# A decay attention with two expert layers on one core: decays first, pads later, one more pair in plain float32

## The chip, the cores and the metric

The kernel runs on one NeuronCore of a Trainium2 chip. The metric is the device time of one execution in microseconds (us), the median of several runs. Engines are named as in the profile: PE is TensorE (PEld its weight load), DVE VectorE, ACT ScalarE, POOL GpSimd, SP SyncE, which here only starts DMAs. ACT starts some DMAs too; the queues of both are SPq and ACTq in the rows.

## The reference

Batch 4, 8 heads, 576 tokens, head width 64; the float64 weights are 512 x 1536 (two), 1536 x 512, 512 x 1024 and 1024 x 512.

```python
log_f = np.log(np.clip(f, 0.0001, 1.0)); cum = np.cumsum(log_f, axis=-1)
scores = scale * q @ k.T + cum[:, :, :, None] - cum[:, :, None, :]
scores = np.where(causal, -1e9, scores)
attn = np.exp(scores - max) ; attn = attn / (attn.sum() + 1e-9)
x = (attn @ v)                                  # to 2304 tokens x 512
h = ((x @ w_a) * (x @ w_b)) @ w_out             # first layer, 512 -> 1536 -> 512
h = h @ w_in                                    # second layer, 512 -> 1024
solu = h * softmax(h)
out = (solu - mean) / sqrt(var + 1e-6) * g_ln @ w_out2
```

## The kernel before, in words

**An order from a planner.** The kernel describes its work as some thousand operations (`op`: allowed engines with planned durations, a key, what it reads and writes, what it must follow in `after`). `Sched.run` places them: of all engines it takes the one that can start something first, and on it the ready operation with the smallest key. The keys come from the table `Y`: `Z0`, `T0`, `T1`, `TA`, `TF` and `ZD` set the time of each head, `W0`, `WD0` and `WK` those of the pieces of weights, `TE`, `T2`, `EO`, `EL` those of the second layer. Every engine then executes its instructions in that order; a wait at the head of an engine or of a DMA queue holds all that stands behind it. Two costs matter below: an operation counts as ready `LAT` = 0.06 us after what it depends on, and a DMA with a key below `D2` may go on SP's or ACT's queue, whichever ends first.

**Decays** (L563 to L591). `f`, 32 rows of 576, is loaded into `ft`, clipped on DVE (L571), its logarithm taken on ACT (L574), summed on DVE (scan L576, with a tile of ones, `on`, from the memset L570), negated (`cumr`, L580) and its low part made (`cl`, L583). For the first three heads a row of each goes by DMA into the head's `sets` (`load_cum`), for the others over DRAM. The scores read these rows as extra lines of the contraction.

**Attention.** A head loads q, k and v (`four_load`, `four_v`, `pair_load`, `late_v`), transposes q and k on PE (L909), splits them in a rounded high part and a low part (L929 to L944, copies L918), and computes each row's maximum from a first product (`max_scores`, L973; with the causal mask either added by a product of `ident` and `cmask` on PE, L977, or added on DVE, L1000; the maximum then comes from L997). Heads below `PM` and those of the first batch mask on PE. A second product (`scores`, L1047 and L1055) then subtracts the maximum, and ACT takes the exponential. Three kinds of heads exist: `K0` (the first 256 queries of the first batch's heads), `K1` (their other 320 queries) and `KF` (whole heads of the other batches). For `K0` and `K1` the exponentials are multiplied with v in plain float32 (`weigh_whole`, L1136). For `KF` the exponentials (L1167) are masked on POOL (L1176), rounded on ACT (L1183), their low part is made on DVE or POOL (L1189), v is split too (`v_split`), and `weigh` (L1224) runs three products for each piece.

**Weights and first layer.** `load_cols` loads float64 weights in pieces into two buffers and converts them on ACT, DVE and POOL (L659 to L706). `up_unit` (L1356) multiplies a block of tokens with one piece of `w_a` and `w_b`, and the products go to DRAM. `down` (L1650) is the second product of the layer.

**Second layer.** `pair` takes 256 tokens and computes `x @ w_in` by seven products of halves (L1736, buffers of one bank in turn out of three), added up on DVE into `h1` (first 128 tokens) and `h2` (L1747). `rest` then does for each: maximum (L1780), exponential (L1782), product, mean and variance, subtraction (L1794), transposes on PE (L1828), the split of the transposes on ACT (L1831) and DVE (L1834), and the product with `w_out2` (L1843), scaled on the way out (L1853). `h1`, `h2` and the transposes have one buffer each.

**Constants and products of zeros.** POOL makes `ident` and `cmask` (L535); `k_set` fills the constant lines of `sets`, part 0 (first 256 columns) and parts 1 and 2, the pads (L523 to L532); `k_nat` (L515) and `k_vs` (L542) are more of them. After planning, `fill` puts products of `ident` and the zeros of `cmask` (L1901) into PE's planned gaps before `F1`, once both are there; their result is used by nothing.

Of the kernel before, what the change touches and what calls it, by code (L numbers as in the profile page):

```python
# [23 lines left out]
def t_act(n, psum=False):  # L24
    return (0.155 if psum else 0.187) + n / 1200.0
# [22 lines left out]
def t_mm4(ns):  # L48
    return sum(n / 600.0 + 0.05 for n in ns)
# [22 lines left out]
class Sched:  # L72
# [21 lines left out]
    def op(self, opts, key, fn, r=(), w=(), after=(), lat=0.0, port=False, nbytes=0, lean="BIAS"):  # L94
# [11 lines left out]
        for b, p in r:  # L106
            if p in b.last:
# [25 lines left out]
    def run(self, state):  # L133
# [70 lines left out]
        while left:  # L204
# [91 lines left out]
    "Z0": 13.6157,  # L296
    "T0": 4.7453,
    "T1": 5.9693,
    "TA": 10.8799,
    "TF": 18.2246,  # L300
    "U0": 2.8496,
    "U1": 1.2595,
    "UF": 2.1602,
    "UL": 1.1171,
    "LEAD": (1.2959, 6.0955),
    "SHRINK": 1.9433,
    "W0": 39.7443,
    "WD0": 3.1311,
    "WN": 4,
    "WD1": 0.0,  # L310
    "WD2": 11.5154,
    "EZ": 8.5785,
    "EO": 17.4803,
    "TE": 28.6422,
    "DL": 0,
    "BIAS": 0.3295,
    "UO": (7.4065, 7.7289, 10.1476),
    "UD": 26.2153,
    "UK": 375.6785,
    "L3": 14,  # L320
    "TL": (0.0, 0.0),
    "F1": 287.7428,
    "FG": 0.275,
    "FF": 0.7369,
# [32 lines left out]
    "WIN": 0.0,  # L357
# [4 lines left out]
def kernel(  # L362
# [154 lines left out]
    op(("POOL", 0.5), 20.0, k_nat, w=[(CONST, "natpad")])  # L517
# [48 lines left out]
    ft, on, cum = xr(0)[:BH], pfw[:BH, :S], xr(1)[:BH]  # L566
# [1384 lines left out]
```

## Time and profile before

| | us |
|---|---|
| median of 3 runs | 911.74 (910.98 to 911.75) |
| the profiled execution | 911.28 |
| its span, first to last instruction | 909.50 |
| PE busy | 891.7 |
| DVE busy | 616.2 |
| ACT busy | 462.5 |
| POOL busy | 169.4 |

The profile is that of one execution. A matmul's end is modelled, and successive matmuls overlap, so a busy PE is not PE at its peak; products of zeros count as busy. In the rows an instruction of a `...ld` engine is a weight load. What stands in brackets is the idle time of the engine just before, and what ended it. In the chain of waits a row is what the end of the program hung on at that time.

### The profile page before, as it was taken

Reading aid. Unit: us, or ns where it says so; the run is one execution under the profiler, and the core shown is the slowest. Engines: PE = TensorE matmul, PEld = TensorE weight load, DVE = VectorE, ACT = ScalarE, POOL = GpSimd, SP = SyncE. Lnnn points to the kernel's source line nnn. Section 1 sums busy time; section 2 is a strip of 40 time slices with the busy share of each in tenths; the row PEclk is TensorE's granted clock in tenths of the full one; section 3 lists DMA queues with packets and bytes.
Section 4 is the critical chain, followed back from the end, with each engine's and each line's share of the span. In section 5 each row is a group of like instructions: output and inputs, shape, how many; then the busy total and the mean of one; then the engine's idle time right before and its main releaser. Section 6 shows DMA issues by size and latency. Waiting matters only on the chain.

```text
span 909.5 us, 14259 instructions
## 1 busy us (share of the span) xinstructions
PE 891.7 (98%) x5027; PEld 764.0 (84%) x5031; DVE 616.2 (68%) x1198; ACT 462.5 (51%) x869; POOL 169.4 (19%) x297
## 2 busy tenths in 40 slices
PE   8999999999999999999999999999999999999996
PEld 4778877999888888888888888988888888888884
DVE  7868767776746656655664345889587768757784
ACT  4967755767564556563663234655333434243332
POOL 7766743222321224111100000000000000000000
PEclk9999999999999999999999999999999999999999
DMA  7446562333333233322484233442120111111001
GB/s 169 129 127 175 154 180 73 90 90 84 90 87 77 75 90 82 96 61 66 139 272 139 67 119 111 156 151 81 47 70 24 46 59 47 35 49 41 28 25 35
DMA packets 110044, 85.02 MB, mean 93 GB/s; under 512 B 69874, under 2 KB 91508, under 8 KB 109972
## 3 DMA queue, kind: packets, MB, share of 16 engines
q1 hardware_dynamic: 106116, 82.11, 31.4%
q10 hardware_dynamic: 3856, 1.99, 0.9%
q8 instruction: 40, 0.66, 0.3%
q14 instruction: 32, 0.26, 0.1%
HBM read 57.38 MB, written 19.55 MB: 85 GB/s over the span
## 4 chain that ended last, share of the span: by engine, by line
PE 93%; ACT 3%; DVE 2%; DMA 1%; issue 1%; POOL 0%; ACTq 0%; DVEq 0%; SPq 0%
PE ps L1356 32%; PE ps L1650 16%; PE ps L1843 11%; PE ps L1736 9%; PE ps L1224 7%; PE ps L1055 3%; PE ps L973 3%; PE ps L1047 3%; PE ps L1136 2%; PE ps L909 2%; PE ps L1828 2%; PE ps L1901 1%; DMA fw<-in_moe_w_a_dram 1%; DVE mts L997 1%; ACT sets L929 0%
## 5 line engine op out<-in xcount | busy, mean ns | idle before, releaser
L1356 PE MATMUL ps<-xs,wt 128*128 128x256 f32 (+1 forms) x1728 | 327.0, 341 | 0.0
L1356 PEld LDWEIGHTS ps<-xs,wt 128*128 128x128 f32 x1728 | 268.0, 189 | 34.0 <-POOL wt L706 0.3
L1650 PE MATMUL ps<-wt,sets 128*128 128x512 f32 (+1 forms) x420 | 91.8, 370 | 0.0
L1650 PEld LDWEIGHTS ps<-wt,sets 128*128 128x128 f32 x420 | 72.9, 189 | 12.8
L1843 PE MATMUL ps<-wt 128*128 128x512 f32 x324 | 80.3, 393 | 1.8 <-DVE wt L1834 1.0
L1381 DVE TENSOR_TENSOR fw<-ps,fw 128x256 f32<-128x256 f32 (+1 forms) x72 | 40.1, 556 | 58.8 <-PE ps L1356 33.4
L1736 PE MATMUL ps<-wt,xs 128*128 128x512 f32 x306 | 79.3, 392 | 0.0
L1189 DVE TENSOR_TENSOR pexp<-fw,pexp 128x768 fp32r<-128x768 f32 (+1 forms) x46 | 46.3, 1007 | 42.6 <-ACT pexp L1183 41.9
L1843 PEld LDWEIGHTS ps<-wt 128*128 128x128 f32 x324 | 60.0, 188 | 15.1 <-DVE wt L1834 1.9
L1224 PE MATMUL ps<-pexp,VS 128*128 128x448 f32 (+4 forms) x432 | 72.2, 312 | 0.4 <-DVE pexp L1189 0.4
L1638 ACT CAST wt<-nat 128x512 fp32r<-128x512 f32 (+1 forms) x60 | 34.7, 580 | 70.4 <-PE ps L1650 66.2
L1224 PEld LDWEIGHTS ps<-pexp,VS 128*128 128x128 f32 x432 | 65.8, 190 | 4.5 <-DVE pexp L1189 0.5
L1736 PEld LDWEIGHTS ps<-wt,xs 128*128 128x128 f32 x306 | 56.5, 188 | 11.4 <-DVE wt L1834 0.2
L1379 ACT COPY fw<-ps 128x256 f32<-128x256 f32 (+1 forms) x72 | 34.6, 480 | 60.8 <-PE ps L1356 59.0
L1176 POOL TENSOR_SCALAR_AFFINE_SELECT fw<-fw 128x128 f32<-128x128 f32 (+1 forms) x120 | 34.6, 319 | 146.1 <-ACT fw L1167 146.0
L1000 DVE CUSTOM_DVE_ANT_0 ps<-ps,cmask 128x512 f32<-128x512 f32 (+4 forms) x95 | 51.0, 554 | 13.7 <-PE ps L973 12.0
L1642 DVE TENSOR_TENSOR wt<-nat,wt 128x512 fp32r<-128x512 f32 (+1 forms) x60 | 38.0, 634 | 28.1 <-ACT wt L1638 26.9
L1167 ACT ACTIVATE fw<-ps 128x768 f32<-128x768 f32 (+1 forms) x48 | 39.7, 836 | 27.7 <-PE ps L1055 25.7
L1047 PE MATMUL ps<-sets 128*128 128x320 f32 (+4 forms) x200 | 49.6, 295 | 1.8 <-DVE mts L997 1.1
L1248 ACT ACTIVATE xrw<-ps 64x576 f32<-64x576 f32 (+2 forms) x40 | 22.0, 550 | 54.4 <-PE ps L1224 52.1
L1055 PE MATMUL ps<-sets 67*128 67x288 f32 (+6 forms) x200 | 48.9, 320 | 0.0
L973 PE MATMUL ps<-sets 66*128 66x512 f32 (+5 forms) x192 | 45.2, 329 | 0.6 <-ACT sets L929 0.3
(186 smaller groups left out, 1518.1 us busy)
## 6 DMA issues: line engine op xcount, KB each, us to landing
gs<-fw SPq DMA_DIRECT2D x36, 256.0 KB
nat<-gs SPq DMA_DIRECT2D x36, 256.0 KB
fw<-in_moe_w_out_dram SPq DMA_DIRECT2D x15, 512.0 KB
sets<-sets SPq DMA_DIRECT2D x48, 144.0 KB
fw<-in_moe_w_b_dram SPq DMA_DIRECT2D x10, 512.0 KB
fw<-in_moe_w_a_dram SPq DMA_DIRECT2D x9, 512.0 KB
nat<-gs SPq DMA_DIRECT2D x36, 128.0 KB
nat<-in_k_dram SPq DMA_DIRECT2D x34, 128.0 KB
```

What stands on the lines that cost most here:

```text
L973: nc.tensor.matmul(bank(ms[part], o, w), lhsT=MB(st)[:D + 2, i * P:(i + 1) * P], rhs=SB(st)[:D + 2, k0:k0 + w], start=True, stop=not pm)
L1000: nc.vector.tensor_tensor_reduce(out=x, in0=x, in1=cmask[:n, off:off + w], scale=1.0, scalar=-3.0e38, op0=ALU.add, op1=ALU.max, accum_out= ...
L1047: nc.tensor.matmul(dst, lhsT=SA(st)[:, ks], rhs=MA(st)[:, q0:q1], start=True, stop=False)
L1055: nc.tensor.matmul(dst, lhsT=SB(st)[:depth, ks], rhs=MB(st)[:depth, q0:q1], start=False, stop=True)
L1167: op(("ACT", t_act(n, True)), key + K.rk[4] + 5.5 + 0.9 * i, lambda i=i, n=n, pf=pf: nc.scalar.activation(out=pf(), in_=bank(ss[i], K.base ...
L1189: o.fn = lambda o=o, bh=bh, bl=bl, n=n, pf=pf: ENG[o.eng].tensor_tensor(out=pexp[:, 64 * bl.slot:64 * bl.slot + n], in0=pf(), in1=pexp[:, ...
L1224: nc.tensor.matmul(bank(u, K.uo + q0, q1 - q0), lhsT=V[:, vp], rhs=src[:, o:o + q1 - q0], start=(k_ in K.first and ip == 0), stop=(k_ in K ...
L1356: nc.tensor.matmul(bank(u[m % len(u)], uo[m], n_), lhsT=wv(m, wp, c)[:, kk], rhs=xsv(i, xx, kk), start=(kk == 0 and n == 0), stop=(kk == K ...
L1381: op(("DVE", t_dve(n_)), key - 50.0, lambda: nc.vector.tensor_tensor(out=gtv(), in0=bank(u[-1], uo[1], n_), in1=atv(), op=ALU.mult), r=[(u ...
L1650: nc.tensor.matmul(bank(py, 512 * d, n), lhsT=WO[c][0][:, wp * DM:(wp + 1) * DM][:, ds_], rhs=ghv(gb, gp)[:, :n], start=(c == 0 and i == 0 ...
L1736: nc.tensor.matmul(bank(bk, 0, 512), lhsT=yc(yx, yp)[:, kk], rhs=wi(wx, wp, kk), start=(n == 0), stop=(n == 5))
L1843: nc.tensor.matmul(bank(po, 0, DM), lhsT=zp[:, c], rhs=w2(c, wp), start=(c == 0 and i == 0), stop=(c == NF2 - 1 and i == 2))
```

## The change

The planner: an operation whose predecessor is on the same engine is ready at its end, without `LAT` (PE and PE alone before); no DMA goes on ACT's queue from the ninth on until the logarithm of the decays (`hold`) is placed; the planned durations of ACT and of plain float32 products change; the table `Y` has new values almost everywhere. The pads, `k_vs` and `k_nat` are made later, and the loads of v and of the second four heads' q and k follow the decays (`CUM`). `on` covers all partitions and serves the early products of zeros. A fourth kind of head, `KE`, is `KF` with the exponentials used as they are: for heads 8 and 9 they are masked on POOL and multiplied in plain float32 with v, which is loaded (`whole_v`) beside columns of ones into `AG` and `nat`. `pair` has, for the last pair alone, another order of the seven products.

```diff
 def t_act(n, psum=False):
-    return (0.155 if psum else 0.187) + n / 1200.0
+    return (0.167 if psum else 0.2) + n / 1200.0
 def t_mm4(ns):
-    return sum(n / 600.0 + 0.05 for n in ns)
+    return sum(n / 600.0 + 0.012 for n in ns)
...
+                    if o.dma and e2 == "ACT" and len(landed) >= 8 and not self.hold.scheduled:
+                        continue
...
-                x.ready = max(x.ready, done + (0.0 if x.opts[0][0] == e == "PE" else self.LAT))
+                same = e != "SP" and not x.dma and not o.dma and all(y[0] == e for y in x.opts)
+                x.ready = max(x.ready, t + dur if same else done + self.LAT)
...
-    "Z0": 13.6157,
-    "T0": 4.7453,
-    "T1": 5.9693,
+    "Z0": 8.6278,
+    "T0": 5.7779,
+    "T1": 5.884,
...
-    "F1": 287.7428,
+    "F1": 255.5172,
...
-    "PM": 13,
+    "PM": 11,
...
-    "WK": (0.0, 1.6676, 0.3157, 0.3157, 0.691, 4.4048, -1.8104, -2.5031, -0.4604, -0.8687, -0.4604, -0.4604, 0.1728, 5.2982, -4.2621, -1.7675, -2.8075, -3.9633, 0.9198, 0.922, 1.6127, 2.3428, -4.0947, -5.0106, 2.9777, -3.4971, 2.7689, -5.9926),
+    "WK": (0.442, 1.6676, 0.3157, 0.5095, 2.8449, 1.5645, -2.071, -3.1521, -7.1043, -8.7374, 2.6109, -10.4068, -5.4567, 6.064, -7.1907, -5.1711, -7.0864, -2.284, 9.5634, 13.177, 3.6127, 5.1046, -1.1177, -12.2003, 19.8573, 8.1844, 17.9519, 4.0211),
...
+    "PO": 1,
+    "TP": 0.0212,
+    "KE": 1,
...
-    "EL": -0.5058,
+    "EL": 10.6117,
...
-    op(("POOL", 0.5), 20.0, k_nat, w=[(CONST, "natpad")])
...
-    ft, on, cum = xr(0)[:BH], pfw[:BH, :S], xr(1)[:BH]
+    ft, on, cum = xr(0)[:BH], pfw[:, :S], xr(1)[:BH]
...
+    MASKS.append(b_on.last[0])
...
-    op(("ACT", 0.69), -3.0, lambda: nc.scalar.activation(out=ft, in_=ft, func=AF.Ln),
+    s_.hold = op(("ACT", 0.69), -3.0, lambda: nc.scalar.activation(out=ft, in_=ft, func=AF.Ln),
...
+    op(("POOL", 0.5), 20.0, k_nat, w=[(CONST, "natpad")], after=CUM)
...
     JOBS = [(t, K0) for t in range(H)] + [(t, K1) for t in range(H)] + [
-        (t, KF) for t in range(H, NH)]
+        (t, KE if t < H + 2 * Y["KE"] else KF) for t in range(H, NH)]
...
-            op(("SP", 0.58), key, lambda c=c: go(c), w=[(nb, c)], nbytes=Y["NB"], lat=2.0)
+            op(("SP", 0.58), key, lambda c=c: go(c), w=[(nb, c)], nbytes=Y["NB"], lat=2.0,
+               after=CUM if t % H else ())
...
-            op(("SP", 0.58), key, lambda h=h: go(h), w=[(nb, h)], nbytes=0.5 * Y["NB"], lat=2.0)
+            op(("SP", 0.58), key, lambda h=h: go(h), w=[(nb, h)], nbytes=0.5 * Y["NB"], lat=2.0,
+               after=CUM)
...
+    def ve(c, h):
+        o = 768 + 192 * c + D * h
+        return AG[:, o:o + P] if c < 4 else nat[:LAST, 2 * NATW + D * h:2 * NATW + D * h + P]
+
+    def whole_v(t, key):
...
+        for h in range(2):
+            op(("SP", 0.58), key, lambda h=h: go(h), lat=2.0, w=[(V5[0], h)], nbytes=131e3, after=K1W)
+        op(("SP", 0.76), key, lambda: go(2), lat=2.0, w=[(V5[1], "V")], nbytes=33e3, after=K1W[:8])
...
-            op(("SP", 0.58 if j < 2 else 0.76), key, lambda j=j: go(j), lat=2.0, after=ROWS[:Y["RW"]] + (K1W[:8] if t == H and nm == "v" else []),
+            op(("SP", 0.58 if j < 2 else 0.76), key, lambda j=j: go(j), lat=2.0, after=ROWS[:Y["RW"]] + (K1W[:8] + KEW if t == H + 2 * Y["KE"] and nm == "v" else []),
...
+            if K is KE:
+                continue
             op(("ACT", t_act(n)), key + K.rk[5] + 6.8 + 0.9 * i, lambda bh=bh, n=n, pf=pf: nc.scalar.copy(
...
-        af = K1W + UPS if i == 2 else ()
+        af = K1W + KEW + UPS if i == 2 else ()
...
+    def pads():
+        op(("POOL", 0.8), 20.5, lambda: k_vs(0), w=[(CONST, "vs0")], after=K0W[:1])
+        op(("POOL", 0.8), 20.6, lambda: k_vs(1), w=[(CONST, "vs1")], after=K0W[:1])
+        for s in range(NSET):
+            o = op([("POOL", 1.0), ("DVE", 1.0)], 20.0, None, w=[(CONST, f"pad{s}a")], after=K0W[:1])
+            o.fn = lambda s=s, o=o: k_set(s, 1, ENG[o.eng])
+            op(("POOL", 0.6), 20.0, lambda s=s: k_set(s, 2), w=[(CONST, f"pad{s}")], after=K0W[:1])
...
-            at_(z - lead - 6.0, lambda: fours.update({(t // 4, "v"): four_v(t, z - lead - 2.5)}))
+            at_(z - lead - 6.0, lambda: fours.update({(t // 4, "v"): four_v(t, z - lead + 6.0)}))
...
+        if first:
+
+            p6 = product("s2", "t2")
+            plus(H["h2", 1], p6, H["h1", 0], (h2, 1), [(h1, 0)], key + 3.0)
+            p2 = product("12", "21")
+            plus(H["h1", 0], p2, H["h1", 0], (h1, 0), [], key + 4.3)
+            p5 = product("s1", "t1")
+            plus(H["h1", 1], p5, H["h2", 1], (h1, 1), [(h2, 1)], key + 5.6)
+            p3 = product("s4", "22")
+            plus(H["h1", 1], p3, H["h1", 1], (h1, 1), [], key + 7.0)
+            p7 = product("s3", "t3")
+            plus(H["h2", 0], p7, H["h2", 1], (h2, 0), [(h2, 1)], key + 8.5)
+            plus(H["h2", 1], p5, H["h2", 0], (h2, 1), [(h2, 0)], key + 8.6)
+            p4 = product("22", "t4")
+            plus(H["h2", 0], p4, H["h2", 0], (h2, 0), [], key + 9.9)
+        else:
...
-    at, todo = max(o.done for o in MASKS) + 0.2, []
+    at, todo = MASKS[2].done + 0.15, []
```

## Rows read from the trace of the kernel before

**Rows 1.** Busy us by stretch: span, then each engine (instructions), PE clock, DMA share, GB/s

```profile
0.00:12.79 12.79, 8.94 (x35) 4.80 (x36) 10.03 (x27) 3.99 (x8) 9.86 (x37) 1.00 0.81 143
12.79:71.50 58.71, 55.92 (x401) 44.06 (x402) 44.05 (x80) 44.91 (x101) 41.22 (x53) 1.00 0.51 141
...
110.00:150.00 40.00, 36.56 (x251) 29.61 (x251) 28.23 (x50) 21.89 (x45) 18.98 (x32) 1.00 0.55 144
150.00:860.00 710.00, 710.00 (x3867) 617.79 (x3868) 470.37 (x925) 346.35 (x620) 74.02 (x153) 1.00 0.29 86
860.00:909.50 49.50, 41.83 (x206) 33.74 (x204) 32.53 (x74) 16.57 (x40) 0.00 (x0) 0.98 0.10 27
```

**Rows 2.** The same view, PE's instructions of L1901 alone

```profile
0.00:12.79 12.79, 7.21 (x21) 1.00 0.81 143
12.79:71.50 58.71, 15.97 (x95) 1.00 0.51 141
110.00:150.00 40.00, 6.24 (x22) 1.00 0.55 144
```

**Rows 3.** Timeline of the first 13 us: start, duration, engine, line, operation

```profile
3.93 0.44 DVE L571 TENSOR_SCALAR xrw<-xrw 32x576 f32<-32x576 f32 x1
...
5.06 0.37 ACTq L442 DMA_DIRECT2D nat<-in_k_dram  x1
...
5.48 0.68 ACT L574 ACTIVATE xrw<-xrw 32x576 f32<-32x576 f32 x1 [3.42 <-DVE sets L524]
...
6.76 0.38 DVE L525 MEMSET sets<- 2x384 f32 x1
...
7.17 1.34 DVE L576 TENSOR_TENSOR_SCAN xrw<-fw,xrw 32x576 f32<-32x576 f32 x1
...
8.76 0.61 DVE L580 TENSOR_SCALAR xs<-xrw 32x576 fp32r<-32x576 f32 x1
...
9.40 0.43 DVE L932 TENSOR_TENSOR sets<-ps,sets 64x256 fp32r<-64x256 f32 x1
...
9.75 0.74 DVE L583 SCALAR_TENSOR_TENSOR xs<-xrw,xs 32x576 fp32r<-32x576 f32 x1
...
12.81 0.47 PE L973 MATMUL ps<-sets 66*128 66x256 f32 x1
```

**Rows 4.** Groups by line, first 12.79 us, DVE: count | busy, mean ns

```profile
L523 DVE MEMSET sets<- 64x384 f32 x2 | 0.8, 378 | 0.2
```

**Rows 5.** Chain of waits: start, duration, engine, line, count; products of zeros

```profile
7.69 2.67 PE ps L1901 x7
...
11.22 0.86 PE ps L1901 x4
```

**Rows 6.** Chain of waits: a K1 head's weighing, half a KF head's, one mask product

```profile
96.95 2.42 PE ps L1136 x12
...
152.06 1.39 PE ps L1224 x9
...
153.57 0.07 PE ps L977
```

**Rows 7.** Chain of waits and, for L1183, timeline: before the first KF weighing

```profile
129.90 5.38 DMA fw<-in_moe_w_a_dram
...
147.12 1.61 ACT L1183 CAST pexp<-fw 128x768 fp32r<-128x768 f32 x2
...
148.80 0.97 DVE pexp L1189
```

**Rows 8.** Chain of waits (a product), then PE's waits after 860: us, times, longest

```profile
873.12 1.36 PE ps L1736 x6
...
PE ps L1828 <- DVE xrw L1794: 1.2, 1, 1.2
...
PE ps L1843 <- DVE wt L1834: 1.0, 1, 1.0
...
PE ps L1843 <- ACT wt L1831: 0.8, 2, 0.4
```

More of the change, by code (lines that the diff above doesn't have):

```diff
@@ L106, in op @@
         for b, p in r:
+            assert p in b.last or b.cls, p
             if p in b.last:
@@ L295 @@
 Y = {
-    "Z0": 13.6157,
-    "T0": 4.7453,
-    "T1": 5.9693,
[L299 to L308, printed above, removed]
-    "WN": 4,
[L310 to L314, printed above, removed]
-    "DL": 0,
[L316 to L320, printed above, removed]
+    "Z0": 8.6278,
+    "T0": 5.7779,
+    "T1": 5.884,
+    "TA": 10.92,
+    "TF": 18.3671,
+    "U0": 3.9329,
+    "U1": 3.2704,
+    "UF": 2.3238,
+    "UL": 1.3336,
+    "LEAD": (1.3468, 6.1224),
+    "SHRINK": 2.3365,
+    "W0": 39.835,
+    "WD0": 3.1123,
+    "WN": 4,
+    "WD1": 0.0081,
+    "WD2": 15.0328,
+    "EZ": 9.4388,
+    "EO": 19.7242,
+    "TE": 28.8271,
+    "DL": 0,
+    "BIAS": 0.6613,
+    "UO": (7.859, 9.2606, 7.5415),
+    "UD": 27.1947,
+    "UK": 414.1889,
+    "L3": 17,
     "TL": (0.0, 0.0),
-    "F1": 287.7428,
-    "FG": 0.275,
-    "FF": 0.7369,
+    "F1": 255.5172,
+    "FG": 0.2449,
+    "FF": 0.6945,
     "RA": 1,
@@ L759 @@
     K0.wp, K0.base = K0.pieces, (0,)
-    for K in (KF, K0, K1):
+    vars(KE).update(vars(KF))
+    for K in (KF, K0, K1, KE):
         K.n = K.q1 - K.q0
@@ L872, in late_v, with go @@
                    w=[(xrb[0, c], ("V", h)) for c in range(4)], nbytes=131e3)
-        op(("SP", 0.76), key, lambda: go(4, 0), lat=2.0, w=[(V4[0], "V")], nbytes=33e3)
+        op(("SP", 0.76), key, lambda: go(4, 0), lat=2.0, w=[(V4[0], "V")], nbytes=33e3, after=K0W[:1])
+    V5, KEW = [], []
+    def ve(c, h):
+        o = 768 + 192 * c + D * h
+        return AG[:, o:o + P] if c < 4 else nat[:LAST, 2 * NATW + D * h:2 * NATW + D * h + P]
+    def whole_v(t, key):
+        if not V5:
+            V5.extend([Buf(None), s_.buf("v5", lambda _: [(0, 2)], "natv")])
+            op(("POOL", 0.45), key, lambda: nc.gpsimd.memset(
+                AG[:, 768:].rearrange("p (c x) -> p c x", c=4)[:, :, D:P], 1.0), w=[(V5[0], "one")], after=K1W)
+            op(("POOL", 0.25), key, lambda: nc.gpsimd.memset(
+                nat[:LAST, 2 * NATW + D:2 * NATW + P], 1.0), w=[(V5[1], "one")], after=K1W[:8])
+        b = t // H
+        LV.append(t // 2)
+        def go(h):
+            if h < 2:
+                issue(
+                    out=AG[:, 768:].rearrange("p (c x) -> p c x", c=4)[:, :, P * h:P * h + D],
+                    in_=v[b, t % H + h, :4 * P].rearrange("(c t) d -> t c d", t=P))
+            else:
+                issue(
+                    out=nat[:LAST, 2 * NATW:2 * NATW + 2 * P].rearrange("p (h x) -> p h x", h=2)[:, :, :D],
+                    in_=v[b, t % H:t % H + 2, 4 * P:].rearrange("h t d -> t h d"))
+        for h in range(2):
+            op(("SP", 0.58), key, lambda h=h: go(h), lat=2.0, w=[(V5[0], h)], nbytes=131e3, after=K1W)
+        op(("SP", 0.76), key, lambda: go(2), lat=2.0, w=[(V5[1], "V")], nbytes=33e3, after=K1W[:8])
     def pair_load(t, nm, src, K, key):
@@ L1142, in weigh_whole @@
                 rv = [(vb, t), (CONST, "ones")]
+            elif K is KE:
+                rv = [(V5[x], y) for x in range(2) for y in ("one", "V" if x else t % 2)]
+                rv += [(P_[part][0], ("f", j)) for j, x in enumerate(K.pieces) if x[1] == part]
             else:
@@ L1246, in out_ @@
         fs = len(s_.ops)
-        late = K1W if K is KF and t < H + 2 else ()
+        late = K1W if t in (H, H + 1) and K is not K1 else ()
         op(("ACT", t_act(n, True)), key + K.rk[8] + 11.5, lambda: nc.scalar.activation(
@@ L1471 @@
     xz = {i: Z[JE[i]] + Y["UO"][0 if i == 0 else 1 if i < 3 else 2] + 2.0 for i in JE}
+    at_(Z[4], pads)
     for j, (t, K) in enumerate(JOBS):
@@ L1684, with pair @@
     s_.cls("sm", 3)
-    def pair(j, t, key, late=0.0):
+    def pair(j, t, key, late=0.0, first=False):
         yb = ends[j]
@@ L1767, in pair @@
         for i, hb in ((0, h1), (1, h2)):
-            rest(j, t + i, hb, hv["h1" if i == 0 else "h2"], key + 9.0 + Y["T2"] * i, late)
+            rest(j, t + i, hb, hv["h1" if i == 0 else "h2"],
+                 key + 9.0 + Y["T2"] * i - (Y["TP"] if first and not i else 0.0), late)
     def rest(j, t, hb, h, k_, late):
@@ L1896, in place, with fill @@
         return (x, True) if next_[x] > 0.0 else None
[L1898 removed]
+    def fill(us, x, alone, early):
+        a, z = (on.bitcast(BF16)[:, :P], on.bitcast(BF16)) if early else (identb, cmask)
         def go():
             for _ in range(int(us / (0.2267 if alone else 0.109))):
[L1901 to L1902 removed]
+                nc.tensor.matmul(ps[:, 512 * x + (0 if alone else 2 * P):512 * x + 512], lhsT=a,
+                                 rhs=z[:, :512 if alone else 2 * P], start=alone, stop=alone)
         return go
[L1905 removed]
+    at, todo = MASKS[2].done + 0.15, []
     for o in order:
@@ L1909 @@
             if gap > Y["FG"] and place(at):
-                todo.append((at, fill(gap * Y["FF"], *place(at))))
+                todo.append((at, fill(gap * Y["FF"], *place(at), at < max(o.done for o in MASKS) + 0.1)))
             at = max(at, o.start + dict(o.opts)[PE])
```

77 lines of the change are left out of this document (39 added, 38 removed), and 26 rows, old and new, of the table Y.

## The prediction

> **What bounds the kernel now.** I read four views in this order. The busy times by stretch come first [rows 1]: the PE column shows where TensorE leaves time. From 150 to 860 us it equals the length of the stretch, so there only less TensorE work can shorten the run. The other four stretches shown fall short by 3.85, 2.79, 3.44 and 7.67 us. Then the same stretches for line 1901 alone [rows 2]: these are the products of zeros, which count as busy and compute nothing, 7.21, 15.97 and 6.24 us. With them 47.2 us of the span hold no useful TensorE work: 11.1 before 12.79 us, 18.8 up to 71.5, 9.7 between 110 and 150, 7.7 at the end. A change outside these four places must cut matmuls; one inside them can win only what the place has.
>
> The timeline of the first 13 us [rows 3] shows a single chain: clip of f (L571), Ln (L574), scan (L576), negation (L580), low part (L583), a DMA of one row into `sets`, and with it the first score matmul at 12.81 (L973). The keys and queries are ready before, so this chain is the bound of the first stretch. The waits of TensorE in the last 50 us [rows 8] sum to 1.2 + 1.0 + 0.8 = 3.0 us; the other 4.7 us of 7.7 lie behind the last matmul (last eviction and store) and nothing here touches them.
>
> The profiled execution took 911.28 us, with a span of 909.50 and 1.78 around it; the median of the runs is 0.46 us higher. I sum against 911.28 and add the 0.46 at the end.
>
> **The change part by part.**
>
> *Decays' chain.* [Rows 3] show three stalls in it. Ln starts at 5.48, 1.1 us after the clip ended (3.93 + 0.44 = 4.37), because ScalarE was issuing a key DMA at 5.06 in front of it (ACTq), one that stood waiting; the change keeps such DMAs off ScalarE's queue until Ln is planned. The scan starts at 7.17, 1.0 us after Ln ended (6.16), behind the memsets of L523 to L525 on VectorE, of which the last runs 6.76 to 7.14; the change puts these pads after the first weighing. The low part starts at 9.75, 0.38 us after the negation ended, with an L932 of another head at 9.40 between them; the planner now lets an operation follow its predecessor on the same engine without the 0.06 us that let L932 slip in. With the clip where it was: Ln 4.42 to 5.10, scan 5.15 to 6.50, negation 0.25 later as now (6.75 to 7.36), low part 7.40 to 8.14 in place of 10.49: 2.35 us sooner. The row's DMA keeps its 2.3 us to the first score. I take **-2.3**. Bounds: 0, if the rows wait behind the other DMAs of their queue; -3.3, if f lands a microsecond before the clip began (VectorE was in memsets until then, so the trace can't show when f was there).
>
> *What is moved.* The pads' memsets run in the first 12 us today: six on VectorE (two sets of L523 to L525; 0.8 us for two of a line [rows 4]), seventeen on GpSimd (the third set, three of L515, nine of L530 to L532, two of L542). Behind them on GpSimd stand the copies L918, on VectorE the chain. At 0.38 each, which most of GpSimd's are smaller than, an estimate of all is 2.3 us on VectorE and at most 6.5 on GpSimd. They go into the stretch from 12.79 to 71.5, where GpSimd is busy 41.2 of 58.7 us and VectorE 44.1 [rows 1], and nothing needs them before the second kind of head. Cover: 17.5 us of idle GpSimd. Without it they cost 8.8 us over three engines, 2.9. I take **+0.5**, near the covered end; bounds 0 and +2.9. The loads of v and of the second four heads now wait for the decays and come after the row DMAs on SP and ScalarE; between the first score and the first weighing lie a maximum, a transpose, the scores and an exponential, in which a load as long as the row's 2.3 us has room. Nothing, or up to +1 if they land late.
>
> *Products of zeros from the first memset.* They may start at the end of `on`'s memset rather than of `cmask`'s. TensorE waits for nothing of theirs. They matter only by the clock: seven of 512 columns take 2.67 us from 7.69, four take 0.86 from 11.22 [rows 5], that is 0.38 us each, mostly the 1.2 GHz level, and then 0.215, the 2.4 GHz one, although the granted clock of the slice reads 1.00. Today the engine is at the upper level when the scores come. With scores at 10.5 us it should be again, since its activity also starts sooner. Nothing; +1, an estimate for two dozen short matmuls at half speed like the L973 of 0.47 us [rows 3], if the first head's products run at the lower level.
>
> *One more pair in plain float32.* Heads 8 and 9 are weighed by 6 products over 1600 columns instead of 18 over 4800. On TensorE a head of the split kind costs 2 x 1.39 = 2.78 us, a head of the second kind 2.42 us for 1216 columns, so 3.18 for 1600 [rows 6]: +0.4 a head, +0.8 in all. The Trainium skill (FP8 and Floating Point Precision, section TensorE Precision Notes) says that true float32 makes four passes through the array; an estimate by that page is 4 x 1600 columns at 2.4 GHz, 2.67 us, 0.1 less than the split head, so it would be -0.2 for the pair. The row has 4.8 columns' time for one column, so I go by the row. These +0.8 fall between 110 and 150 us, where 9.7 us are free of work: nothing, +0.8 without that cover. What goes: four casts on ScalarE (1.61 for two, 3.2 in all) and four subtractions of 0.97 on VectorE [rows 7], and the pair's split of v. Its gain is in the chain: today the first such head can be weighed after cast and subtraction, at 148.80 + 0.97 = 149.77; without them at 147.12, where the cast starts: 2.65 us sooner. TensorE lacked work for only 9.7 of the 40 us of that stretch, so at least a quarter of it, 0.65, is won, at most all. I take the middle, **-1.6**. Late next is the load that arrives at 135.3 after 5.38 us [rows 7] with ScalarE waiting for it; the pair does not touch that. Two extra memsets and the wait of the next pair's v for this pair's weighing are covered by the 10.9 us planned for a head.
>
> *Masks.* `PM` from 13 to 11 takes the mask products off TensorE for heads 11 and 12: five each, at 0.07 us [rows 6], ten times 0.07, **-0.7**, in the stretch that TensorE fills. VectorE masks instead; it has a third of its time free there (470 of 710 us busy [rows 1]). Bounds 0 and -0.7.
>
> *Last pair's order.* The last pair's first half is complete after five products instead of seven: two of 1.36 us [rows 8], 2.7 us sooner, and its chain of softmax and normalization with it. That chain is what TensorE waits for: 1.2 us at the transposes (L1828 for L1794), then 0.8 and 1.0 at L1843. Sooner by 2.7, the transposes stand behind products that are still running and the 1.2 go. Of the 1.0 (VectorE in the other half's chain when it should split) I count half; the 0.8 are the hand-over after each transpose and stay unless other products are left, which the later key `EL` (10.6) of the pair before may provide. I take **-1.8**; bounds -3.0 and 0. The new order sends the second product's sum into `h2`, which the pair before frees only by its transposes: if it waits there, the gain is eaten.
>
> *Planner's costs and keys.* They change the order everywhere, with no work added. Between 150 and 860 us no gap can be closed; in 12.79 to 71.5 and 110 to 150 they can win or lose. I take 0, bounds -8 and +6 (the 9.7 us less my 1.6; one more wait as long as the 5.38).
>
> Sum: -2.3 + 0.5 - 1.6 - 0.7 - 1.8 = -5.9; 911.28 - 5.9 = 905.4, and on the scale of the median **905.8 us**.
>
> **Rivals.**
>
> *B, the free stretch closes.* With less work on the three engines and new priorities, 110 to 150 us loses most of its 9.7 us: 5 more than my 1.6. For: ScalarE, the engine that waits there, is busy only 21.9 of 40. Against: its wait is for a load, and loads are not faster. 900.8 us.
>
> *C, the head start is not passed on.* From 12.79 to 71.5 the three other engines are busy 41 to 45 of 58.7 us, each by its order, and TensorE does little; if weight conversions set the pace there, scores that start 2.3 us sooner only wait longer. For: 16 us of products of zeros in that stretch. Against: the weights wait for the decays too, and so start sooner. 905.8 + 2.3 = 908.1 us.
>
> *D, slower.* The weights' keys move by up to 20 us for single pieces (from the 16th on), most of them later. TensorE then waits between 110 and 150 for pieces that were there: each such wait costs what the present one took, 5.4 us, and ScalarE, which works in order, holds the heads' chain behind it. One eats the gain (911.2), two give 916.6; it decides from more than one. For: the trace has that wait already. Against: the converters are free a third of the time.
>
> *N, it doesn't do what it says.* Chain and tail keep their length because the first DMAs and the `h2` buffer take the places of the old waits; what is left is +0.5 - 1.6 - 0.7: 909.9 us.
>
> **How the numbers follow.** Forecast 0.42 (904 to 907.5), B 0.16, C 0.20, N 0.09, D 0.13. About 0.2%, 1.8 us, is what a measurement of this kernel can tell from no change: the bounds are 909.9 and 913.6. Faster: 0.42 + 0.16 + nearly all of C + half of N = 0.80; same: the other half of N, a little of C and a fifth of D, 0.09; slower: the rest of D, 0.11. The range leaves out the far side of B and the worse part of D: 899.5 to 912.0.
>
> **What would show it.** Right: Ln within 0.1 us of the clip's end; scan, negation and low part back to back; first L973 near 10.5 us; 55 instead of 65 matmuls of L977; L1136 up by 24 instructions and L1224 down by 36; less of L1901 in total; waits of TensorE in the last 50 us near 1.2. Wrong: a first score at 10.5 with the first of the second kind of heads no sooner than today (C); new waits of ScalarE or GpSimd for `in_moe_w` loads after 100 us (D); any gap between 150 and 860 us; L1747 of the last pair waiting for L1828.

## The result and the profile after

The changed kernel took 904.11 us at the median of four runs (902.68 to 904.15), the kernel before 911.36 beside it: ratio 0.9918, 95% interval 0.9901 to 0.9935. Five more runs on another chip (experiment after_again) gave 903.25 (902.56 to 906.34), ratio 0.9922 (0.9908 to 0.9937). The forecast was 905.8, so sign and range held; the time came out 1.7 us below it, and the gain is 7.2 us where 5.9 was forecast. The profiled execution took 904.06, 7.22 less than the one of before, with a span of 902.3.

Line numbers have moved: products of zeros are L1978 (L1901 before), score matmuls L1008 (L973), masks by TensorE L1012 (L977), plain float32 weighing L1171 (L1136), split weighing L1269 (L1224), products of the last pair L1793 (L1736), its last matmuls L1917 (L1843).

The same stretches as in [rows 1], all engines (span, then busy us of PE, PEld, DVE, ACT, POOL, PE clock, DMA share, GB/s), of the changed kernel:

```profile
0.00:12.79 12.79, 9.52 (x47) 4.86 (x48) 9.14 (x25) 4.68 (x10) 6.83 (x24) 1.00 0.43 91
12.79:71.50 58.71, 56.43 (x405) 46.23 (x407) 47.09 (x84) 47.09 (x106) 39.67 (x62) 1.00 0.56 150
71.50:110.00 38.50, 38.38 (x266) 32.15 (x264) 30.94 (x48) 29.36 (x57) 21.17 (x23) 1.00 0.62 171
110.00:150.00 40.00, 38.79 (x252) 30.98 (x253) 26.47 (x56) 24.82 (x52) 21.69 (x40) 1.00 0.58 155
150.00:860.00 710.00, 707.38 (x3839) 615.56 (x3839) 481.71 (x948) 337.33 (x606) 61.26 (x144) 1.00 0.29 86
860.00:902.30 42.30, 36.07 (x171) 28.97 (x169) 25.77 (x56) 13.15 (x32) 0.00 (x0) 1.00 0.09 25
```

And the products of zeros alone (PE, PEld), which answer [rows 2]:

```profile
0.00:12.79 12.79, 6.91 (x22) 2.35 (x22) 1.00 0.43 91
12.79:71.50 58.71, 11.04 (x58) 5.36 (x61) 1.00 0.56 150
71.50:110.00 38.50, 0.79 (x2) 0.20 (x2) 1.00 0.62 171
110.00:150.00 40.00, 4.65 (x17) 1.70 (x19) 1.00 0.58 155
```

Idle time plus products of zeros is the time in which TensorE does nothing useful. Up to 150 us it was 10.08 + 29.42 = 39.5; now it is 6.88 + 23.39 = 30.3: **9.2 us gained**. In the tail idle time went from 7.7 to 6.2, **1.4 gained**. From 150 to 860, where [rows 1] had no gap, there is one now, **2.6 lost**. Useful work went from 862.3 to 863.2, **0.85 lost**. That is -9.2 - 1.4 + 2.6 + 0.85 = -7.2, the whole difference of the two spans.

The decays' chain, timeline, against [rows 3] (start, duration, engine, line, operation; idle before it and releaser in brackets):

```profile
4.00 0.44 DVE L572 TENSOR_SCALAR xrw<-xrw 32x576 f32<-32x576 f32 x1
...
4.47 0.68 ACT L575 ACTIVATE xrw<-xrw 32x576 f32<-32x576 f32 x1 [2.39 <-DVE xrw L572]
...
5.19 1.35 DVE L577 TENSOR_TENSOR_SCAN xrw<-fw,xrw 32x576 f32<-32x576 f32 x1 [0.75 <-ACT xrw L575]
6.57 0.47 DVE L581 TENSOR_SCALAR xs<-xrw 32x576 fp32r<-32x576 f32 x1
7.08 0.83 DVE L584 SCALAR_TENSOR_TENSOR xs<-xrw,xs 32x576 fp32r<-32x576 f32 x1
...
9.96 0.36 PE L1008 MATMUL ps<-sets 66*128 66x256 f32 x1 [0.88 <-DMA sets<-xs]
```

Each link starts within 0.05 us of the end of the one before; the first score comes at 9.96 in place of 12.81, and TensorE waited 0.88 us for its row. In the kernel before the score at 12.81 had no idle time of TensorE in front of it: products of zeros ran up to it, and the chain of waits goes through them [rows 5]. That the decays set this start is therefore shown by the runs that move their chain, below, and not by [rows 3].

The new gap, TensorE's timeline at 570 us:

```profile
569.78 4.96 PE L1401 MATMUL ps<-xs,wt 128*128 128x256 f32 x40
576.29 0.73 PE L1793 MATMUL ps<-wt,xs 128*128 128x512 f32 x2 [1.55 <-ACT xs L1757]
578.10 2.07 PE L1793 MATMUL ps<-wt,xs 128*128 128x512 f32 x4 [1.07 <-DVE xs L1761]
```

In the kernel before, twelve products of the `down` loop stood between the last L1356 and the first product of the first pair, while ScalarE and VectorE split its inputs:

```profile
584.36 2.91 PE L1650 MATMUL ps<-wt,sets 128*128 128x512 f32 x12
587.11 1.52 PE L1736 MATMUL ps<-wt,xs 128*128 128x512 f32 x6
```

In the new order nothing stands there. Behind the gap the granted clock falls (span, PE busy, clock):

```profile
570.00:580.00 10.00, 7.38 (x47) 0.89 0.38 128
580.00:590.00 10.00, 10.00 (x43) 0.94 0.29 100
```

### The profile page after: what moved, and what is told of

Its sections match the earlier page's. It is cut to its first block, busy times and chain, and to the rows that moved or that the text cites. A ratio compares the mean times of both kernels' runs of the same rounds, so it can differ in the third digit from the quotient of the medians.

```text
span 902.3 us, 14146 instructions
## 1 busy us (share of the span) xinstructions
PE 886.6 (98%) x4968; PEld 758.8 (84%) x4973; DVE 621.1 (69%) x1214; ACT 456.4 (51%) x859; POOL 150.6 (17%) x293
## 4 chain that ended last, share of the span: by engine, by line
PE 92%; DVE 4%; ACT 1%; issue 1%; POOL 0%; DMA 0%; DVEq 0%; ACTq 0%; POOLq 0%
PE ps L1401 33%; PE ps L1707 16%; PE ps L1917 10%; PE ps L1793 9%; PE ps L1269 6%; PE ps L1090 3%; PE ps L1008 3%; PE ps L1171 3%; PE ps L1082 3%; PE ps L944 2%; PE ps L1902 2%; DVE mts L1032 1%; PE ps L1978 0%; PE ps L1050 0%; PE ps L1012 0%
## 5 line engine op out<-in xcount | busy, mean ns | idle before, releaser
L1401 PE MATMUL ps<-xs,wt 128*128 128x256 f32 (+1 forms) x1728 | 323.7, 340 | 0.1
L1793 PE MATMUL ps<-wt,xs 128*128 128x512 f32 x306 | 78.8, 394 | 2.6 <-ACT xs L1757 1.6
L1917 PE MATMUL ps<-wt 128*128 128x512 f32 x324 | 79.6, 394 | 1.5 <-ACT wt L1905 1.4
L1917 PEld LDWEIGHTS ps<-wt 128*128 128x128 f32 x324 | 59.7, 188 | 14.7 <-ACT wt L1905 1.8
L1035 DVE CUSTOM_DVE_ANT_0 ps<-ps,cmask 128x512 f32<-128x512 f32 (+4 forms) x105 | 56.5, 555 | 22.1 <-PE ps L1008 19.6
L1793 PEld LDWEIGHTS ps<-wt,xs 128*128 128x128 f32 x306 | 57.4, 190 | 14.9 <-ACT xs L1757 1.8
L1269 PE MATMUL ps<-pexp,VS 128*128 128x448 f32 (+4 forms) x396 | 64.8, 311 | 0.0
L1269 PEld LDWEIGHTS ps<-pexp,VS 128*128 128x128 f32 x396 | 59.5, 190 | 3.5
L1008 PE MATMUL ps<-sets 66*128 66x512 f32 (+3 forms) x192 | 44.3, 332 | 2.9 <-DVE mts L1032 1.1
```

The costliest lines, as they stand in the source:

```text
L1008: nc.tensor.matmul(bank(ms[part], o, w), lhsT=MB(st)[:D + 2, i * P:(i + 1) * P], rhs=SB(st)[:D + 2, k0:k0 + w], start=True, stop=not pm)
L1035: nc.vector.tensor_tensor_reduce(out=x, in0=x, in1=cmask[:n, off:off + w], scale=1.0, scalar=-3.0e38, op0=ALU.add, op1=ALU.max, accum_out= ...
L1269: nc.tensor.matmul(bank(u, K.uo + q0, q1 - q0), lhsT=V[:, vp], rhs=src[:, o:o + q1 - q0], start=(k_ in K.first and ip == 0), stop=(k_ in K ...
L1401: nc.tensor.matmul(bank(u[m % len(u)], uo[m], n_), lhsT=wv(m, wp, c)[:, kk], rhs=xsv(i, xx, kk), start=(kk == 0 and n == 0), stop=(kk == K ...
L1793: nc.tensor.matmul(bank(bk, 0, 512), lhsT=yc(yx, yp)[:, kk], rhs=wi(wx, wp, kk), start=(n == 0), stop=(n == 5))
L1917: nc.tensor.matmul(bank(po, 0, DM), lhsT=zp[:, c], rhs=w2(c, wp), start=(c == 0 and i == 0), stop=(c == NF2 - 1 and i == 2))
```

## Experiments

Where a granted clock of 1.000 over the whole run is named, spans of such runs alone are compared: the kernel before took 908.0 to 910.4 in its twenty-three, the changed one 900.8 to 901.5 in its four, 901.15 in the mean.

**The changed kernel again**, to be compared on one chip with the first three below.

> The changed kernel once more, beside the three edited forms of it on the same chip. All theories: 904.1 us again, 7.3 less than before, first score matmul near 10.0 us and two waits of TensorE at 576 to 578 us, 2.6 together.

903.25 us as told above. The first score and both waits were there (1.6 and 1.1 us).

**Is the head start passed on?** First in the changed kernel, by delaying its chain.

```
-    op(("DVE", 0.45), ..., lambda: nc.vector.tensor_scalar(out=ft, in0=ft, ...
+    def clip():
+        for _ in range(7):
+            nc.vector.tensor_scalar(out=ft, in0=ft, scalar1=1.0e-4, scalar2=1.0, ...
...
+                if todo and o is first and not longer:
+                    gap += 2.64 / Y["FF"]
```

> Only the decays' chain of the changed kernel is made later: the clip of f is done seven times in place of once, six more at 0.44 us, 2.64 us in all, and the products of zeros ahead of the first score are longer by the same time, so that TensorE does not rest more than it did. No order changes. Theory (the chain bounds the start, and what it wins reaches the end): first score near 12.6 us and the end at 904.1 + 2.6 = 906.7. Rival C of the prediction (the other engines set the pace up to 71.5 us, the head start is not passed on): first score near 12.6 as well, the end at 904.1 to 904.6.

905.83 us (905.37 to 908.35), ratio 0.9951 (0.9937 to 0.9965). Timeline of the delay and of the first score:

```profile
4.47 2.86 DVE L574 TENSOR_SCALAR xrw<-xrw 32x576 f32<-32x576 f32 x6
...
12.82 0.36 PE L1011 MATMUL ps<-sets 66*128 66x256 f32 x1 [1.04 <-DMA sets<-xs]
```

The chain and the first score are 2.86 us later. At a clock of 1.000 the three spans are 903.6 to 904.1, 2.7 above the changed kernel's. What the chain loses at its start is lost at the end: rival C falls for the changed kernel.

Then in the kernel before, by moving its chain alone, its planned order kept otherwise.

```
+    for i, o in enumerate((SC, NG, LW)):
+        o.start = LN.start + 0.001 * (i + 1)
...
+    for i in (0, 1, 4, 5):
+        ROWS[i].start = at0 + 0.001 * i
...
+            if 5.0 < at < 11.0:
+                gap *= 0.45
```

> The kernel before with one part of the change by hand, its planned order kept otherwise: Ln ahead of the key DMA on ScalarE, scan, negation and low part back to back, the first rows' DMAs ahead of the loads of v on SP, the six memsets of L523 to L525 on VectorE behind the first weighing, and the products of zeros from the memset of ones on, with about 2.5 us fewer of them between the chain and the first score. Theory (the chain alone is worth what the prediction gave it): first score near 10.5 in place of 12.81, the end 2.3 us sooner, 908.5 where before takes 910.8. Rival C (the other engines set the pace up to 71.5 us): first score near 10.5, the end within 0.5 of before. Rival (moved work comes back as a wait): first score no sooner than 12, the end within 0.5 of before or later.

911.67 us (910.11 to 914.29), ratio 1.0004 (0.9991 to 1.0018): nothing gained. Timeline of its first score, a weight conversion on ScalarE and the second weighing (L1139 is L1136 of before):

```profile
10.27 0.47 PE L976 MATMUL ps<-sets 66*128 66x256 f32 x1
...
18.13 0.67 ACT L662 ACTIVATE fw<-fw 128x512 f32<-128x512 f32 x1 [1.34 <-DMA fw<-in_moe_w_b_dram]
...
18.95 0.48 ACT L1115 ACTIVATE xrw<-ps 128x384 f32<-128x384 f32 x1
...
19.88 0.92 PE L1139 MATMUL ps<-xrw,fw 128*128 128x256 f32 x4 [1.52 <-ACT xrw L1251]
```

The first score is 2.54 us sooner than in [rows 3]. The second weighing was at 20.38 before, so 0.5 of it is left there: ScalarE waits for a piece of weights, with the head's own exponential (L1115) behind it. So this edit is worth nothing in the old order, where delaying the chain costs 2.7 in the new one. Whether that piece of weights is the cause:

```
+    first = [o for o in order if o.dma and any(b.cls == "raw" for b in o.bufs)][:2]
+    first[0].start, first[1].start = min(first[0].start, 5.5456), at0 + 0.006
```

> chain_only with two DMAs more moved: the first pieces of in_moe_w_a (ScalarE's queue, issued at 10.35 us there) and in_moe_w_b (SP's, 12.48, behind the four loads of v) go out right behind the decays' row DMAs. Theory (in before's order the head start is lost because ScalarE, which works in order, stands at 15.74 and 18.13 for these two pieces with the first heads' copies behind it): the waits of ScalarE at L674 and L662 for these DMAs go, the second weighing comes near 17.9 in place of 19.88, and the end is 1.5 to 2.3 us sooner than before, 908.8 to 909.6 on the scale of 911.1. Rival (the next pieces stop it in the same way, or the loads of v come late now): the end within 0.5 of before.

910.73 us (909.49 to 915.01), ratio 1.0005 (0.9995 to 1.0015): the theory of the two pieces falls. At a clock of 1.000 its four spans are 907.8 to 908.9, those of the nine of before beside it 908.2 to 910.4; that is 0.7 in the mean, with ranges that overlap. The two waits of ScalarE are gone and the second weighing comes at 18.36, 2.0 sooner than before. What comes next is VectorE:

```profile
15.84 0.38 DVE L523 MEMSET sets<- 64x384 f32 x1
...
18.09 0.38 DVE L525 MEMSET sets<- 2x384 f32 x1
...
19.95 0.62 DVE L1000 TENSOR_REDUCE mts<-ps 128x1 f32<-128x256 f32 x2
```

```profile
20.63 0.38 PE L1018 MATMUL ps<-ident,mts 128*1 128x128 f32 x2 [1.35 <-DVE mts L1000]
```

And the same maximum in the kernel before:

```profile
19.47 0.62 DVE L997 TENSOR_REDUCE mts<-ps 128x1 f32<-128x256 f32 x2
```

The six memsets that the edit puts behind the first weighing take VectorE from 15.84 to 18.47 here and from 15.32 to 17.95 in chain_only, two weight conversions follow, and the third head's maximum starts at 19.95 and 19.94, later than in the kernel before. TensorE waits 1.35 for it. So both runs move the pads together with the chain, and what the head start would be worth in the old order without them is not shown. In the changed kernel these memsets also run on VectorE, between 15.46 and 18.37, but there the second head's maximum stands ahead of them, at 11.44, and its weighing is not held up:

```profile
15.43 0.89 PE L1171 MATMUL ps<-xrw,fw 128*128 128x256 f32 x4
```

**The pair in plain float32.** First its chain made long again, nothing planned around it:

```
             if K is KE:
+                again = lambda pf=pf: nc.scalar.copy(out=pf(), in_=pf())
+                larger = lambda pf=pf: nc.vector.tensor_tensor(out=pf(), in0=pf(), in1=pf(), op=ALU.max)
+                EXTRA.append((bf, again, larger))
                 continue
...
```

> The changed kernel with the chain of the pair in plain float32 made as long as the split pair's was: for each of its four halves a copy of the exponentials onto themselves on ScalarE and a maximum of them with themselves on VectorE between mask and weighing, 0.8 and 0.97 us each by the rows of before; TensorE's order and products stay. Theory (that chain is worth the middle of the bounds): +1.6 against the changed kernel, waits of TensorE for these tiles between 110 and 150 us. Rival (the stretch has so much planned ahead that it hides them): within 0.3. Rival (it is worth its whole length): +2.65 or more.

912.77 us (908.64 to 916.69), ratio 1.0020 (1.0004 to 1.0036), slower than before. The largest of TensorE's waits in its fastest run (us, times, longest):

```profile
PE ps L1171 <- DVE fw L1228: 5.1, 3, 2.2
```

That run, at a clock of 1.000, has a span of 906.9, 5.7 above the changed kernel's. The other runs show clocks down to 0.987 and spans up to 915.0. The whole-length rival is nearest, and even it is exceeded: three of the four halves wait, not one. No order was planned for this longer chain, and the additions also take 3.4 us of ScalarE and 4.0 of VectorE, so 5.7 is more than the chain would cost in an order of its own.

Then the pair weighed in the split kind, with numbers adapted to it:

```
-    "KE": 1,
+    "KE": 0,
...
```

> The changed kernel with heads 8 and 9 weighed in the split kind again (KE 0 in place of 1), and the numbers of the table Y, second layer's included, adapted to that, since the changed numbers are fitted to the pair in plain float32; TensorE's work is 0.8 us less. Theory of the prediction (the pair's chain is worth 1.6 us): about 905.7 where the changed kernel takes 904.1 at the median of its nine runs so far. Theory from casts_back (it is worth the 5.1 us of waits that appear when the chain is made long again and nothing is planned around it): 908 to 909. Rival (with numbers of its own the split kind is as good): 903.3 to 904.5.

907.37 us (906.00 to 908.37), ratio 0.9952 (0.9936 to 0.9968); at a clock of 1.000 spans of 904.2 and 904.3, 3.1 above the changed kernel's. From 110 to 150 us, all engines (columns as in the first fence) and the products of zeros alone:

```profile
110.00:150.00 40.00, 37.84 (x263) 31.81 (x261) 31.65 (x57) 24.51 (x48) 20.75 (x36) 1.00 0.55 149
```

```profile
110.00:150.00 40.00, 5.83 (x23) 1.98 (x23) 1.00 0.55 149
```

Idle time and products of zeros up to 150 us are 8.86 + 25.97 = 34.8, 4.6 more than the changed kernel's. So the pair is worth about 3.1 at the end, between the two theories. The numbers of the table are others in this run and less finely fitted than the changed kernel's, so 3.1 is rather too much than too little.

Where it gains is told by TensorE's largest waits from 71.5 to 150 us. The kernel before, where the pair is split as well:

```profile
PE ps L1023 <- DVE mts L997: 1.3, 1, 1.3
PE ps L1047 <- DVE mts L997: 1.1, 1, 1.1
PE ps L1224 <- DVE pexp L1189: 0.4, 1, 0.4
```

And pair_split:

```profile
PE ps L1058 <- DVE mts L1032: 1.0, 1, 1.0
PE ps L1008 <- DVE mts L1032: 0.6, 1, 0.6
```

For the pair's own subtraction TensorE waits 0.4 us before and not at all in pair_split. It waits for the maxima that VectorE computes: 2.4 before, 1.6 in pair_split, 0.6 in the changed kernel. From 110 to 150 us VectorE is busy 31.65 of 40 with the split pair, 26.47 without. This points to VectorE's time, and not to the length of the pair's chain; no run takes the two apart.

**The last pair's order.**

```
-    "PO": 1,
+    "PO": 0,
```

> The changed kernel with the last pair's products in the order of before (the key PO 0 in place of 1); nothing differs ahead of 850 us. Theory: the waits of TensorE in the last 50 us grow from 1.4 us back to near the 3.0 of before, +1.6, the end at 905.7. Rival (the later key EL and the new order of the pair before removed the wait, the product order does nothing): 904.1 to 904.4.

907.18 us (906.27 to 907.41), ratio 0.9956 (0.9943 to 0.9968), 3.9 above after_again on the same chip, where 1.6 was expected. TensorE's timeline in its tail, and the clock there:

```profile
882.52 1.09 PE L1902 MATMUL ps<-ident,xrw 128*128 128x128 f32 x8 [1.31 <-DVE cmask L1873]
884.22 1.22 PE L1917 MATMUL ps<-wt 128*128 128x512 f32 x2 [0.60 <-ACT wt L1905]
885.69 6.38 PE L1917 MATMUL ps<-wt 128*128 128x512 f32 x16 [0.25 <-DVE wt L1908]
```

```profile
880.00:890.00 10.00, 7.84 (x26) 5.47 (x25) 9.03 (x24) 3.59 (x9) 0.00 (x0) 0.71 0.07 26
```

And the same place in after_again:

```profile
884.47 1.03 PE L1902 MATMUL ps<-ident,xrw 128*128 128x128 f32 x8
886.38 0.73 PE L1917 MATMUL ps<-wt 128*128 128x512 f32 x2 [0.89 <-ACT wt L1905]
887.27 3.92 PE L1917 MATMUL ps<-wt 128*128 128x512 f32 x16 [0.15 <-DVE wt L1908]
```

The wait at the transposes is back, 1.31, as the theory says. Most of the rest is the clock: the sixteen products behind the waits take 6.38 in place of 3.92, 2.5 more, and 1.31 + 2.5 make 3.8 of the 3.9. All five runs have clocks of 0.995 to 0.998. The kernel before had the same wait of 1.24 in its profiled run without such a fall; why there not, stays open.

**The rests.**

```
+        if 300.0 < at < 800.0 and o.start - at > 3.0:
...
+            for _ in range(22):
+                nc.tensor.matmul(ps[:, 512 * x:512 * x + 2 * P], lhsT=identb, ...
```

> The changed kernel with 22 products of 256 columns, about 2.4 us of TensorE at the 0.11 us that such a product takes, in the place where it waits at 576 to 578 us for the first pair's inputs; their results are used nowhere. Theory (the rest lets the granted clock fall, which shows 0.89 and 0.94 in the two slices of 10 us behind it, 1.7 us in all): the clock stays at 1.00 there, the last wait still ends near 578, and the end comes 1.3 to 1.7 us sooner, 902.4 to 902.8. Rival (only the wait itself costs, the lower clock is hidden or comes from elsewhere): 904.1, within 0.3.

902.98 us (902.84 to 906.02), ratio 0.9918 (0.9904 to 0.9932). Two stretches of its profiled run, span 904.3:

```profile
10.00:15.00 5.00, 4.72 (x27) 3.64 (x27) 1.68 (x6) 1.75 (x5) 0.26 (x2) 0.70 0.80 174
15.00:20.00 5.00, 5.00 (x27) 4.34 (x27) 3.56 (x10) 2.82 (x8) 4.22 (x17) 0.62 0.62 172
...
580.00:590.00 10.00, 9.53 (x45) 7.59 (x43) 8.83 (x21) 6.82 (x15) 0.61 (x1) 1.00 0.41 134
```

No fall behind 576 us now, but one that follows the rest ahead of the first score, 1.05 us in this run: 3.0 us above this version's three runs at 1.000 (901.1 to 901.5), which are no faster than the changed kernel's, since the gap itself stays. Inconclusive by the median; so both rests were filled:

```
+                if todo and o is first and not longer:
+                    gap += 0.7 / Y["FF"]
...
```

> The changed kernel with products of zeros in the two places where it rests longest: three more of 512 columns in the 0.88 us ahead of the first score, and the 22 products of 256 columns at 576 us. Theory (the spread of the changed kernel, 902.6 to 906.3, comes from clock falls behind these two rests): granted clock 1.00 in nearly all runs, the median at 902.8 or lower and none above 904. Rival (the falls come at any short wait): the spread stays, median 903.0 to 904.0.

902.94 us (902.67 to 903.05), ratio 0.9907 (0.9891 to 0.9923). All five runs have a clock of 0.999 or 1.000 and spans of 900.9 to 901.3, where five of the changed kernel's nine runs took more than 904. The theory holds for the clock and the spread, which came from falls behind these two rests; the median is 0.14 above its 902.8. It is the steadiest version here, as fast as the changed kernel at full clock and 1.1 below the median of its nine runs; the intervals of the two ratios overlap.

Last, with eleven numbers of the second layer changed on top:

> The kernel with both rests filled and eleven numbers of the table Y for the second layer changed (WD2, YC, TE, T2, EZ, EO, EL, TP, XL, UL, UD), so that the small waits of TensorE at 590 to 600 us and the order of the last products differ; nothing differs ahead of 300 us. Theory (the waits that are left there and in the tail are 1.5 us by their rows and can be planned away): the end at 901.5 to 902.3 where rests_filled takes 902.9. Rival (they only change places): 902.7 to 903.5.

902.82 us (902.62 to 903.01), ratio 0.9913 (0.9900 to 0.9926): the rival, no gain that can be told. Behind 160 us TensorE's waits are the same as with both rests filled: 1.4 us at the last matmuls (L1917) and 0.5 at the first pair (L1793).

**Numbers without edits, and the early products.** The changed code with the numbers of before:

```
-    "Z0": 8.6278,
-    "T0": 5.7779,
+    "Z0": 13.6157,
+    "T0": 4.7453,
...
```

> The changed kernel's code with all the numbers of the table Y that before had (only the three new ones PO, TP and KE are added). Theory (what the first 150 us gained beyond the head start and the pair's chain came from the new numbers, and the code by itself needs numbers fitted to it): not faster than before, 911 or more. Rival (the edits carry the gain whatever the numbers): 905 to 908.

927.65 us (927.35 to 929.22), ratio 1.0182 (1.0163 to 1.0201): 16 us slower than before. TensorE is idle for 8.8 us between 150 and 860, where the kernel before was never idle, and the clock of the runs is 0.988 to 0.990. Its largest waits there are 2.9 us for a maximum of VectorE (L1035) and 2.7 for the first pair's inputs (L1757).

Edits and numbers are one thing here: under numbers fitted to other code the same edits lose. The rival (the edits carry the gain whatever the numbers) falls.

The early products of zeros:

```
-    at, todo = MASKS[2].done + 0.15, []
+    at, todo = max(o.done for o in MASKS[:2]) + 0.2, []
...
```

> The changed kernel with the early products of zeros taken out: none before the identity and the mask are written, so five of 512 columns fewer ahead of the first transposes; nothing else differs. The prediction's step (they only start the clock sooner and the engine is at the upper level anyway): within 0.3 of the changed kernel's 903.3 to 904.1, first score near 10.0. Rival (without them the first head runs at the lower level): products of 512 columns ahead of the first score at 0.38 to 0.43 us each in place of 0.22, the end 1 us later or more.

905.37 us (903.58 to 906.76), ratio 0.9941 (0.9929 to 0.9953); the profiled run had a span of 904.6 at a clock of 0.997. That is 1.3 above the changed kernel's nine-run median of 904.06; the interval overlaps both of the changed kernel's a little. TensorE's timeline up to the first score:

```profile
7.67 4.26 PE L1978 MATMUL ps<-cmask,ident 128*128 128x512 bf16 x11
11.58 0.47 PE L1008 MATMUL ps<-sets 66*128 66x256 f32 x1
```

And the same eleven products in the changed kernel:

```profile
6.54 2.54 PE L1978 MATMUL ps<-cmask,ident 128*128 128x512 bf16 x11
```

They take 0.39 us each in place of 0.23, as the rival said, although the granted clock of these slices reads 1.00 in both runs. The first score stands behind them in TensorE's order and comes at 11.58, 1.62 later than in the changed kernel, with the decays' chain at the same place (low part from 7.06, 7.08 there). The rest of this run's 3.4 us above 901.15 comes with a clock of 0.83 from 580 to 590 us, behind the same waits at 576. The one run at a clock of 1.000 has a span of 901.8, only 0.7 above, so not every run loses as much at its start.

## Why the prediction was right, and where its sizes were off

By stretch the forecast had -3.4 for the first 150 us, where -9.2 came; -0.7 for TensorE's work, where +0.85 came; nothing between 150 and 860 us, where +2.6 came; and -1.8 for the tail, where -1.4 came. That these add up to -7.2 against its -5.9 is in part luck: one miss of 5.8 us and others of 4.6 in all went against each other.

- *Bound of the first stretch*: right. The chain did what the terms said and 0.5 more: 2.85 sooner in place of 2.3, each link at the end of the one before. That it reaches the end is shown by chain_late, but only for the new order. In the old one the chain and the moved pads together are worth nothing (chain_only). The prediction took the term as the edit's own; it depends on the order as well.
- *What is moved*, +0.5: not tried alone. In chain_only and chain_loads the six memsets on VectorE are not covered: the third head's maximum behind them comes 0.5 later than before, although the first score is 2.5 sooner. That is nearer to the prediction's price without cover, 2.9.
- *Pair in plain float32*: the mis-sized term, -1.6, where pair_split has up to 3.1. The step that failed is the path. The prediction let the first weighing wait for cast and subtraction until 149.77; by the trace two of its products ran at 149.11, ahead of the subtraction's end, and TensorE waited 0.4 us for it. In the chain of waits the subtraction at 148.80 follows on VectorE's L944 and not on the cast, so VectorE was what it waited for:

```profile
148.01 0.76 DVE sets L944
```

```profile
149.11 0.34 PE L1224 MATMUL ps<-pexp,VS 128*128 128x128 f32 x2
```

  What TensorE waited for in that stretch were VectorE's maxima, 2.4 us, and 0.6 now. That the freed VectorE is the reason is what the rows suggest; it was not tried apart. The size on TensorE was right, as the chain of waits of the changed kernel shows for one head, 3.24 against the 3.18 worked out from [rows 6]:

```profile
133.72 1.37 PE ps L1171 x6
135.97 1.87 PE ps L1171 x6
```

- *Last pair*: right in mechanism. The wait at the transposes is gone, and TensorE's waits in the tail went from the 3.0 of [rows 8] to 1.4 (0.9 and 0.5 for ScalarE's split behind the transposes): 1.6 of the 1.8, and near the 1.2 that was to be seen. That the old order would cost 3.9 with the new numbers, by the clock, was not seen.
- *Planner and keys at 0*, and "between 150 and 860 us no gap can be closed": true, but one was opened, and a gap there was one of the prediction's own signs of being wrong. 2.6 us of wait came at 576, and in the profiled run a fall of the clock behind it: with both rests filled and the clock at 1.00, useful work is 889.58 - 25.73 - 2.58 = 861.3, 1.9 less than the profiled 863.2. The first 150 us made that good: of the 9.2 us gained there the chain (2.7 by chain_late) and the pair (at most 4.6 by the same sums) make 7.3; the other 1.9 are not told apart.
- *Masks*: not tried alone. TensorE's L1012 fell from 65 to 55 as said.
- *Zeros at 0, bound +1*, because "TensorE waits for nothing of theirs": without the early ones it does. In the profiled run of fill_old the later ones ran slower and held up the first score by 1.6 us. So the head start needs the early ones. Its bound of +1 does not follow from its numbers either: two dozen products that lose half of 0.47 us each are 5.6.
- *Rivals*: B's sign was right for its stretch, 110 to 150, where idle time and zeros went from 9.7 to 5.9, 3.8 in place of 1.6. C falls in the new order; in the old one the head start is lost, but memsets on VectorE lie in its way as well as weight conversions. D and N did not happen.

## What to carry to other kernels

A head start is worth what the order behind it lets through: delay the chain by a known amount in the finished kernel before booking it as gain. When moving a chain by hand, look where the work went that made room for it; here six memsets stood in front of the next maximum. Before pricing a chain, read what TensorE waits for: here 0.4 us for the chain that was priced, and 2.4 for another engine's maxima. Behind a wait of TensorE look at the granted clock of the slices that follow; filling the two longest waits with products that nobody uses cost nothing here and made the time repeatable. Such products stand in the engine's order, though, and a slow stretch of them can hold up the real ones.

## What the runs showed of the hardware

The granted clock fell after rests that look alike in some runs and not in others: behind the 2.6 us at 576 it was 0.89 and 0.94 in one run, 0.92 and 0.74 in another (after_again, span 904.6), 1.00 and 0.83 in a third (fill_old), and 1.00 in two more with the same wait (chain_late, old_product_order). Behind the rest of 1.05 us ahead of the first score it was 0.70 and 0.62 once (gap_filled). Against the spans at 1.000 (901.15 in the mean of the changed kernel, 901.3 of gap_filled), such a fall cost 1.2 us (902.3), 3.4 (904.6) and 3.0 (904.3). While the one in the tail lasted (old_product_order), products of 512 columns took 6.38 / 16 = 0.40 us each in place of 3.92 / 16 = 0.245. If all of them took twice 0.245 at the 1.2 GHz level, which is an estimate, most of them ran at it.
